# First two projections of v as fp32 products of raw weights, and a new order of all jobs, in a fused attention and MLP block on one core

## The chip, the cores and the metric

The kernel runs on one core of one Trainium2 chip. The metric is the time of one execution on the device, in microseconds (us). TensorE (PE in the profile) multiplies, VectorE (DVE), ScalarE (ACT) and GpSimd (POOL) work element by element, and SyncE (SP) issues nearly all transfers. TensorE writes into PSUM, which the program uses as eight banks of 128x512 fp32, the tiles `dense0` to `dense7`.

## The reference

For x of 2048 rows and 512 columns the output is the sum of three terms; xn is x normalized over each row.

```python
xn = layernorm(x)
return x + A(xn, wq, wk, wv, wo, beta) + B(xn, w1, b1, w2, b2)

# A: 32 heads of 16 columns, 4 segments of 512 rows
q, k, v = xn @ wq, xn @ wk, xn @ wv
for s in range(4):
    p = softmax(q_s @ k_s.T * scale + causal mask)
    o = g * (phi(q_s) @ M) / (phi(q_s) @ z + 1e-6) + (1 - g) * (p @ v_s)
    M += phi(k_s).T @ v_s ; z += sum(phi(k_s))
return concat(o) @ wo

# B: an MLP of width 1792 with a normalization of its own
return gelu(layernorm(xn) @ w1 + b1) @ w2 + b2
```

## The kernel before

**Products in pieces.** A product of fp32 matrices is done in fp16 as three products (`split3`): each operand is scaled by a power of two and split into a high and a low fp16 half, and high times high, high times low and low times high are summed. For K = 512, four blocks of 128, one such product is 12 matmuls. Before a weight can be used it goes through a chain: a load (`w_load`, job `wl`), a measure of its size (`w_square`, job `wm`: for q, k, v and parts of w1 and w2 a product of the weights' upper 16 bits with themselves on TensorE, line L385), a scale worked out of it (`w_scale`, job `wf`, lines L399 and L415), and the split (`w_split`, job `ws`). Of v, pieces 0 and 1 are loaded by one transfer into the room of the later split pieces (the tile `wvs`), and pieces 2 and 3 by two more into a staging tile `pt`.

**The rows.** Blocks of 128 rows are normalized in fp32 (job `X`), transposed on TensorE (`turn`, line L568), and copied out as two fp16 halves, the tile `xnT`. For the first 256 rows there is besides an fp32 copy of the transposed rows, times 1024, in the tile `hzs[1]` (it shares its room with `hT1`): `ln_first`, job `Xf`, copies block 0 by DVE and block 1 by ACT. It serves the first products for k and q (`qk_proj` with `begin`, jobs `Tp 1` and `Tp 0`, line L621), which use raw weights and are scaled afterwards (`qk_first`).

**The products of v.** `v_nat(s, b)`, job `V`, makes v for the 128 rows of block b of segment s: `split3` over the fp16 halves of rows and weights (12 matmuls of 512 columns at line L602), and a copy by ACT into the tile `vt` with a fixed scale (line L723).

**Filler.** 24 jobs `W` (`warm`, line L503) are two matmuls each of an identity matrix with itself, 256 columns wide, whose result nobody reads. They stand at places of the order at the start.

**The order.** All work is cut into 1762 jobs. The string `ORDER` names for each place the stream whose next job comes there, and `BANKS` the PSUM bank of each tile in turn. The jobs are issued in that order, so each engine executes its instructions in the order of the string, and waits only by semaphores for what its instructions need. SP's transfers go through eight semaphores in rotation: a transfer is issued only when the one that used the same semaphore eight transfers ago has landed.

Of the kernel before, what the change touches and what calls it, by code (L numbers as in the profile page):

```python
# [19 lines left out]
P = 128  # L20
D = 512
KT = D // P
# [7 lines left out]
F = 1792  # L30
# [29 lines left out]
def streams():  # L60
# [77 lines left out]


ORDER = (  # L140
    "auhhwhhhlkhhkhhbth7cdaegi7%ghhhbglhf7fh%klhnhs898hkxvhhc%ekhmhd9j&gh9&,&&%gmffn99h9R3gi9R!xrj!((!o!(y()z*CzD+,"
    "))*BCA,)Y)Y+*P-#)-B+-.)*YDo+Y!Y-Y$Y#p-FFF/Z0yz1z$pF-4.-2o0#1F/RBRA2.0:/B1FF2:QF55Y0./FF:5:5Y5513!>F>:254P55>$;"
    ">FFF55;E5GGq>5Y?HGGF3;YHGFHa<5F@II;I?q[IU?GFbGYYF=GG<yHcFGdFYHze;?Hf?Q;IFEUZCzYY=0D14YI3iI<A?2=IJBGGGKYLB0CH1f"
    "GG;MYDHY@PNH2F<F]IOIa=QI]IFFG0?555512FG0G[1YGF5b5FGF@2H]yHZcHYzFBdF0IIze4II55f5F5[BY@[EA1f2J0Y1]5j2KYL55GFG50Y"
    "1GFG2Y50HFFGY1PZ^HMN52FFFHO5y55zz50AQIII^IFFG55a55G_Fb1GC5^iFGEGY5DDHcH55TIiH20I^II1JVGWGYyBP{BY2KG0GzXLMY55NH"
    "1FFG5_Hz5AOCHDUIIDI201IGT2eF55YFGG5YGHFHGHYFF{IIIIFFF55JZ55B0d1fKfB5RFLR5250EMNRFFGOSFGHG1RGG2HFjY0YHIa1bIQIIG"
    "GFSG6F2FPHyG3FcFHSGFzVQIHI4II5zFS6J0W1UB55KYYCLEDXGG3BDYYT55GAMG2VG55HWYN65PH5HIOIIIFeGXF4U55GG5ZH5FFYY3F0GiF5"
    "y1FGdzFzCY20FF1DHIHIBD42IIf01YJ5YYAF2KBY5501555ZT20L15fE2Y055GGF51YFM2GF5555FHN0GHGYFHFI1IQIOIGF63FYY2GFGYHG0V"
    "FGPHy4WaYFII1HIIJ2QZ5055E5zz55XAjK5GGCBGLHMGD1GH5D5Tb55N55BHIOIIIVGG5Yy2GcWFzYGFdYUGXFYPFH0FzH1IHIeIIFF2ABR0RF"
    "1FFfCJ5RD52FfDK5TREjY0155LGGBGY2MHYN5GFGO5SFHFFIZIUHIQIS0G61aFVbi2G50YW15SFG3YP5FFGyFHzG2Uc6F55CSFEXHzDHIQBID0"  # L150
    "eII143d52JTK5YBYGGY5L50GAMGG5HH5N1YH5O624IIIIGF55FGVFY5GHGyWGFF55XPz55BFHFF5Z0H5CD1Y2FFI0IIQB12zIJ0f1U5F6DY5T5"
    "A2KYY3LY0Y12EGFG5M5GFNF55GVFUYZjW5ifY53H5P50YH5OGFF55H1201IIIIXGFFyF2FGC05G12Gz0G5D55F14HY2YHY5HYYZE5D5I4III01"
    "GG250BJKT5LMYYBj55GGGHN1H5H55YFFFIOIIIY2FFGyFzGGYFGFY0HHYGHVFFIQIIZIJC1R5W20FKR515D5XRL5EBUMDT5NGGG205BOSGFFHS"
    "H1FGFHRFF63IIIIGFF2SGVHFGWXyCGH0zUFG1YD65F55555H5SBI2IIED0ITGGHJYK4LYGGM1BGY6YYYNFHFIIHO20IIFVFG555yWFGG1z553H"
    "56GHGFCFZH4FIII20DB1IFX20F355B5JD5YK551525FYYY05YL1YY20MZ15EF2FTG555051GFNG45HOY2FG55GHFFY01HII2IIGFF50515GGF2"
    "H5YG3FG0Y5FHYY12YIZEHII012IG55015J25KG54LGGHM55GNHV5H5OIIIIGWG555GGH0G51H55H5205I12III5JXK5L5555M5N5555OSS6SS6"
    "66"
)


BANKS = (
    "01234567012345670156721657243657435244521654126547302651473026514302561743025613025461372546172354672436517243"
    "06517240362450137524013752031652031467530124763051276340512463052134061352403524075216470521674032164705271064"
    "25710642570165742316574216574031746035720365470347651063547305642713054672130546721304271635046237156024371564"
    "30275162743051260743162074316203120741307413250741653012756301257630125763051724350172501725316754203705432154"
    "70326471503647105437610243716052416035271603457126045712634012563715263471564372156437241560372415602413652413"
    "06524310675243105672431052467045621720415642015620514320561740561743107526104326143726547324657324650246520453"
    "71024573102457312046312573461527340627135436257106257106257301625430162547316254370431625034176240137652407652"
    "04136240173625401732654012736540127365014273654273016427301247013254613720546137205641205637526031753216053216"
    "0532415630415643107546321065341605347165304716054316054732160457162045371625370162534701"  # L170
)


# [13 lines left out]
def infini_mixer_kernel(ctx: ExitStack, tc: tile.TileContext, x, wq, wk, wv, wo, beta, w1, b1, w2, b2, out):  # L187
    nc = tc.nc
    V, A, G, T, Q = nc.vector, nc.scalar, nc.gpsimd, nc.tensor, nc.sync
# [13 lines left out]
    def dense():  # L203
        return dps.tile([P, 512], F32, name="dense" + next(banks), bufs=1)
# [57 lines left out]
    def col(j):  # L262
        return sc[:, j:j + 1]
# [4 lines left out]
    def flat(m):  # L268
        return WT[m].rearrange("p n a c -> p (n a c)").bitcast(F32)

    def piece(m, c):
        n = PIECES[m]
        return flat(m)[:, 512 * c + 1024:512 * c + 1536] if c < n - 2 else stage[m][c - n + 2]
# [115 lines left out]
    def exponents(dst, x):  # L389

        V.tensor_scalar(dst.bitcast(I32), x.bitcast(I32), 1, 0x7F800000, op0=OP.logical_shift_right, op1=OP.bitwise_and)

    def power(dst, h, sign, e):

        V.tensor_scalar(dst.bitcast(I32), h.bitcast(I32), sign, e << 23, op0=OP.mult, op1=OP.add)

    def qk_scale(g0, n):
        p = dense()
        T.matmul(p[:, :2], ones, am[:, :2 * NG].rearrange("p (w g) -> p w g", w=2)[:, :, g0:g0 + 1], start=True, stop=True)  # L399
        h = p[:, 4:6]  # L400
        exponents(h, p[:, :2])
        h = h.unsqueeze(2).to_broadcast([P, 2, n])
        f, s, c = (qksc[:, j, :, g0:g0 + n] for j in range(3))
        power(s, h, -1, 203)
        power(f, h, 1, 64)
        power(c, h, 1, 41)
        V.scalar_tensor_tensor(qkcs[:, g0:g0 + n], f[:, 0], float(2 ** -16), f[:, 1], op0=OP.mult, op1=OP.mult)

    def w_scale(m):
        if m in ("qk", "QK"):  # L410
            return qk_scale(*((0, 1) if m == "qk" else (1, NG - 1)))
        h = m[1:] == "b"
        n = 4 if h else 3 if m == "o" else 1
        p = dense()
        T.matmul(p[:, :n], ones, am[:, AM[m]:AM[m] + n], start=True, stop=True)  # L415
        if m == "1a":
            T.matmul(p[:, 1:2], ones, am[:, 16:17], start=True, stop=True)
        a = p[:, 6:8]
        r = p[:, :1]
        if n > 1:  # L420
            r = a[:, 1:2]
            V.tensor_reduce(r, p[:, :n], axis=AX.X, op=OP.add)
        exponents(a[:, 0:1], r)
        f, s = {"v": (FV, SV), "o": (FO, SO), "1": (F1 + h, S1 + h), "2": (F2 + h, S2 + h)}[m[0]]
        power(col(s), a[:, 0:1], -1, 203)
        power(col(f), a[:, 0:1], 1, 64)
        if m == "o":
            V.scalar_tensor_tensor(col(CO), col(FO), float(2 ** -20), col(FV), op0=OP.mult, op1=OP.mult)
        elif m[0] == "1":
            power(col(CG + h), a[:, 0:1], 1, 41)  # L430
            if not h:
                exponents(a[:, 1:2], p[:, 1:2])
                power(col(FB), a[:, 1:2], 1, 64)
            V.scalar_tensor_tensor(col(B1F + h), col(f), 23.0, col(FB), op0=OP.mult, op1=OP.add)
            b = col(B1F + h).bitcast(I32)
            V.tensor_scalar(b, b, 0x7F800000, None, op0=OP.bitwise_and)
            power(col(SHH + h), col(B1F + h), -1, 267)
        elif m[0] == "2":
            V.scalar_tensor_tensor(col(C2 + h), col(f), float(2 ** -26), col(B1F + h), op0=OP.mult, op1=OP.mult)
# [17 lines left out]
    wqs, wks, wvs, wos, w2s = (WT[m] for m in "qkvo2")  # L457

    FV, SV, FO, SO, CO = range(5)
    F1, S1, F2, S2, CG, SHH, C2, B1F = range(5, 21, 2)  # L460
    FB = 21

    stats = cst.tile([P, 4, 4, 2], F32, name="stats")
    G.memset(stats, 0.0)
# [129 lines left out]
    def x_cols(s, b, k, u):  # L594
        return xnT[:, (2 * s + b // 2) % 3, k, u, P * (b % 2):P * (b % 2) + P]

    def split3(p, ws, xs):

        i = 0
        for k in range(KT):  # L600
            for a, b in ((0, 0), (0, 1), (1, 0)):
                T.matmul(p, ws(k, a), xs(k, b), start=i == 0, stop=i == 3 * KT - 1)  # L602
                i += 1
# [113 lines left out]

    def v_nat(s, b):
        p = dense()
        split3(p, lambda k, a: x_cols(s, b, k, a), lambda k, a: wvs[:, k, a, :])  # L720
        t = vts[b]
        t4 = t.rearrange("p a (b c) -> p a b c", b=3)
        A.activation(t4[:, :, 0:3:2, :], p.rearrange("p (a b c) -> p a b c", b=2, c=DH), AF.Copy,  # L723
                     scale=float(2 ** -16))
        vt[s, b] = t

    def kv(i):
# [161 lines left out]
    hzs = [t.rearrange("p f a c -> p f (a c)").bitcast(F32) for t in hTs]  # L889
# [131 lines left out]
    def e_of(j, a, f):  # L1021
# [12 lines left out]
        "e": e_of,  # L1034
        "A": lambda tok, k: (acc_load, acc_add)[k](tok),
        "wl": w_load, "par": small_loads, "par2": small_use, "zero": zeros, "hold": hold, "const": consts, "wm": w_square, "wf": w_scale, "ws": w_split,
    }
    A.preload_act_table_set("natural_log_exp_and_others")
# [32 lines left out]
```

## Time and profile before

| | |
|---|---|
| time, median of 3 runs (lowest, highest) | 685.41 us (683.58, 686.34) |
| the profiled execution: its own time | 684.2 us |
| its span, first to last instruction | 682.2 us |
| PE busy | 674.6 us, 99% of the span |
| DVE, ACT, POOL busy | 504.9, 492.4, 376.7 us |

The profile is of one execution. Busy of an engine is the time in which it has an instruction under way; matmuls overlap, so that the start of one matmul to the start of the next is a better measure of its cost than its own duration. A line such as L602 is a line of the kernel's file. In the changed file lines from 430 on are 2 higher, and lines after `v_nat` 7 higher.

### The profile page before, as it was taken

Reading aid. Unit: us, or ns where it says so; the run is one execution under the profiler, and the core shown is the slowest. Engines: PE = TensorE matmul, PEld = TensorE weight load, DVE = VectorE, ACT = ScalarE, POOL = GpSimd, SP = SyncE. Lnnn points to the kernel's source line nnn. Section 1 sums busy time; section 2 is a strip of 40 time slices with the busy share of each in tenths; the row PEclk is TensorE's granted clock in tenths of the full one; section 3 lists DMA queues with packets and bytes.
Section 4 is the critical chain, followed back from the end, with each engine's and each line's share of the span. In section 5 each row is a group of like instructions: output and inputs, shape, how many; then the busy total and the mean of one; then the engine's idle time right before and its main releaser. Section 6 shows DMA issues by size and latency. Waiting matters only on the chain.

```text
span 682.2 us, 15538 instructions
## 1 busy us (share of the span) xinstructions
PE 674.6 (99%) x5683; PEld 381.5 (56%) x5683; DVE 504.9 (74%) x1553; ACT 492.4 (72%) x903; POOL 376.7 (55%) x635
## 2 busy tenths in 40 slices
PE   7999999999999999999999999999999999999997
PEld 6765565666555565655455555564655446465543
DVE  5789989987795768887595875997377676878542
ACT  3588999787775659579846848777868565868970
POOL 5386778655645436564743555535553544466662
PEclk8999999999999999999999999999999999999999
DMA  8977342313122141412212224221501323240101
GB/s 280 256 222 170 113 117 66 95 55 73 48 49 71 40 119 36 124 47 50 72 46 56 64 76 97 73 63 32 118 16 35 79 63 80 70 104 17 18 1 61
DMA packets 52887, 55.81 MB, mean 82 GB/s; under 512 B 4990, under 2 KB 41868, under 8 KB 52812
## 3 DMA queue, kind: packets, MB, share of 16 engines
q1 hardware_dynamic: 50508, 50.64, 26.8%
q0 software_dynamic: 2304, 4.20, 3.8%
q8 instruction: 44, 0.72, 0.4%
q14 instruction: 31, 0.25, 0.1%
HBM read 37.77 MB, written 17.05 MB: 80 GB/s over the span
## 4 chain that ended last, share of the span: by engine, by line
PE 97%; DVE 1%; POOL 1%; DMA 0%; issue 0%; ACT 0%; POOLq 0%; DVEq 0%
PE dense L602 40%; PE dense L951 21%; PE dense L832 11%; PE dense L798 6%; PE dense L756 6%; PE dense L971 6%; PE dense L698 2%; PE dense L568 1%; PE dense L385 1%; PE dense L675 1%; PE dense L733 1%; PE dense L503 1%; PE dense L621 1%; DMA xt<-in_A_x_dram 0%; PE dense L769 0%
## 5 line engine op out<-in xcount | busy, mean ns | idle before, releaser
L763 DVE CUSTOM_DVE_ANT_0 dense<-dense,mask 128x384 f32<-128x384 f32 (+3 forms) x512 | 234.3, 522 | 35.2 <-PE dense L756 34.0
L805 ACT ACTIVATE pt<-dense,qkcs 128x512 f32<-128x512 f32 (+1 forms) x384 | 205.4, 624 | 38.1 <-PE dense L798 37.3
L951 PE MATMUL dense<-w2s,hT 128*128 128x512 f16 x672 | 162.9, 380 | 0.0
L602 PE MATMUL dense<-xnT,w1s 128*128 128x256 f16 x1344 | 159.6, 273 | 0.0
L819 POOL TENSOR_SCALAR_AFFINE_SELECT pt<-pt 128x256 f32<-128x256 f32 x256 | 99.0, 419 | 98.8 <-ACT pt L805 98.6
L602 PEld LDWEIGHTS <-w1s 128*128 128x128 f16 x1344 | 128.7, 98 | 29.8 <-issue 8.6
L925 POOL TENSOR_TENSOR hT<-hh,hT 128x512 f16<-128x512 f32 x64 | 67.2, 1050 | 86.9 <-ACT hT L923 85.0
L951 PEld LDWEIGHTS <-hT 128*128 128x128 f16 x672 | 61.3, 98 | 70.6 <-issue 12.9
L832 PE MATMUL dense<-pt,vt 128*32 128x512 f32 (+3 forms) x1024 | 77.6, 436 | 0.0
L763 DVE DVE_READ_ACCUMULATOR2_ANT mc<- 128x1 f32 x512 | 71.1, 139 | 0.1
L904 DVE SCALAR_TENSOR_TENSOR hT<-dense,sc,cb 128x512 f32<-128x512 f32 x64 | 43.4, 679 | 25.4 <-PE dense L602 24.1
L798 PE MATMUL dense<-qst,kst 50*128 50x384 f16 (+3 forms) x512 | 55.0, 298 | 0.0
L832 PEld LDWEIGHTS dense<-pt,vt 128*32 128x32 f32 x1024 | 31.5, 109 | 40.6 <-issue 28.5
L756 PE MATMUL dense<-kst,qst 48*128 48x384 f16 (+3 forms) x512 | 53.1, 298 | 0.0
L921 POOL TENSOR_SCALAR hh<-hT,sc 128x512 f32<-128x512 f32 x64 | 42.5, 663 | 17.4 <-ACT hT L911 10.4
L911 ACT ACTIVATE hT<-hT,b1t 128x256 f32<-128x256 f32 x112 | 46.9, 496 | 1.9 <-DVE hT L904 1.4
L923 ACT ACTIVATE hT<-hh 128x512 f16<-128x512 f32 x64 | 37.0, 578 | 12.1 <-POOL hh L921 12.1
L971 PE MATMUL dense<-wos,oT 128*128 128x512 f16 (+2 forms) x204 | 44.0, 367 | 0.8 <-DVE acc L973 0.7
L602 PE MATMUL dense<-wvs,xnT 128*128 128x512 f16 x192 | 43.7, 379 | 0.0
L602 PE MATMUL dense<-xnT,wks 128*128 128x512 f16 (+1 forms) x240 | 43.0, 331 | 0.0
L602 PE MATMUL dense<-xnT,wqs 128*128 128x512 f16 (+1 forms) x240 | 43.0, 331 | 0.0
L955 DVE SCALAR_TENSOR_TENSOR acc<-dense,sc,acc 128x512 f32<-128x512 f32 x32 | 23.9, 747 | 19.3 <-PE dense L951 19.0
(227 smaller groups left out, 865.4 us busy)
## 6 DMA issues: line engine op xcount, KB each, us to landing
kst<-kd SPq DMA_DIRECT2D x32, 192.0 KB
qst<-qd SPq DMA_DIRECT2D x32, 192.0 KB
qd<-hl SPq DMA_DIRECT2D x36, 128.0 KB
kd<-hl SPq DMA_DIRECT2D x33, 128.0 KB
acc<-in_A_x_dram SPq DMA_DIRECT2D x16, 256.0 KB
acc<-in_B_b_dram POOLq DMA_DIRECT2D x16, 256.0 KB, 4.2
out_dram<-acc SPq DMA_DIRECT2D x15, 256.0 KB
xt<-in_A_x_dram SPq DMA_DIRECT2D x14, 256.0 KB
```

The source lines that it names most:

```text
L602: T.matmul(p, ws(k, a), xs(k, b), start=i == 0, stop=i == 3 * KT - 1)
L756: T.matmul(p[:, o:o + n], stk[i, 0][r, t, P * qb:P * qb + P], stk[i, 1][r, t, :n], start=True, stop=True)
L763: V.tensor_tensor_reduce(p[:, o:o + n], p[:, o:o + n], mask[:, 512 - n:], 1.0, -3e38, OP.add, OP.max, mc[i][:, 4 * b + t, qb:qb + 1])
L798: T.matmul(p[:, o:o + n], stk[i, 1][r, t, P * kb:P * kb + P], stk[i, 0][r, t, P * kb:], start=True, stop=True)
L805: A.activation(pt[i, 4 * b + t][:, OFF[kb]:OFF[kb] + n], p[:, c:c + n], AF.Exp, scale=qkcs[:, i % NG:i % NG + 1])
L819: G.affine_select(v, v, pattern=[[0, 2], [1, P]], compare_op=OP.is_ge, fill=0.0, base=0, channel_multiplier=-1)
L832: T.matmul(p[32 * c:32 * c + 32, P * kb:], vt[s, kb][:, 4 * g + c, 16 * odd:16 * odd + 32], pt[i, 2 * c + odd][:, OFF[kb]:OFF[kb] + LEN[kb ...
L904: V.scalar_tensor_tensor(hz[:, f0:f + 1, :], p[:, :256 * n].rearrange("p (f c) -> p f c", f=n), col(CG + fh), cbt[hf].unsqueeze(1).to_broa ...
L911: A.activation(hz[:, f, :], hz[:, f, :], AF.Gelu_apprx_tanh, bias=b1t[:, fo:fo + 1])
L925: G.tensor_tensor(hT[:, z, 1, :], hht[j, c], hT[:, z, 0, :], op=OP.subtract)
L951: T.matmul(p, t[:, u, P * a:P * a + P], w2s[:, fo, v, :], start=fi == 0 and n == 0, stop=fi == FH - 1 and n == 2)
L971: T.matmul(p[:, c], o[:, u, P * b:P * b + P], wos[:, g, v, c], start=i == 0, stop=i == 3 * NG - 1)
```

## The change

It has two parts. For segment 0 and blocks 0 and 1 `v_nat` no longer uses split weights and split rows: it multiplies the fp32 copy of the rows in `hzs[1]` with the raw fp32 weights of v, four fp32 products of 512 columns for each block, and the copy by ACT scales with a column `SVT`, which `w_scale` works out for v by one more small instruction of DVE. The weights of v are still split, for the other 14 blocks. And `ORDER` and `BANKS` are replaced throughout: the same jobs, as many of each kind, in another order.

```diff
 ORDER = (
-    "auhhwhhhlkhhkhhbth7cdaegi7%ghhhbglhf7fh%klhnhs898hkxvhhc%ekhmhd9j&gh9&,&&%gmffn99h9R3gi9R!xrj!((!o!(y()z*CzD+,"
+    "auhhwhhhlkhhkhhbth7cdhhlhhhhxhih7hehg%kkfhg%f7ja8kg8bcl9%i9smv9R&9d9he9m&nRnh9fh&r!(%jf(g(!(!ggo)yz),)&*C,#)+D"
...
@@ w_scale
-        if m == "o":
+        if m == "v":
+            power(col(SVT), a[:, 0:1], -1, 187)
+        elif m == "o":
...
-    FB = 21
+    FB, SVT = 21, 22
...
     def v_nat(s, b):
         p = dense()
-        split3(p, lambda k, a: x_cols(s, b, k, a), lambda k, a: wvs[:, k, a, :])
+        first = s == 0 and b < 2
+        if first:
+            for k in range(KT):
+                T.matmul(p, hzs[1][:, k, P * b:P * b + P], piece("v", k), start=k == 0, stop=k == KT - 1)
+        else:
+            split3(p, lambda k, a: x_cols(s, b, k, a), lambda k, a: wvs[:, k, a, :])
...
-                     scale=float(2 ** -16))
+                     scale=col(SVT) if first else float(2 ** -16))
```

**TensorE, from the transposition of the first block to the first product for k.** In the rows below the line is followed by what is written and read; `ident` alone is filler (L503 before, L505 after), `xt` the rows, and L385 the measures of weights. Of several equal rows one or two stand. Before:

```order
L503 MATMUL dense1_187<-ident_74 128x256
L568 MATMUL dense2_200<-ident_74,xt_134 128x128 x4
...
L385 MATMUL dense3_211<-wvs_102 128x128
...
L568 MATMUL dense4_220<-ident_74,xt_136 128x128 x4
...
L503 MATMUL dense5_226<-ident_74 128x256
...
L503 MATMUL dense7_232<-ident_74 128x256
L621 MATMUL dense0_242<-hT1_130,wks_101 128x256 x4
```

After:

```order
L505 MATMUL dense3_233<-ident_74 128x256
L570 MATMUL dense4_236<-ident_74,xt_134 128x128 x4
...
L385 MATMUL dense5_242<-wvs_102 128x128
...
L505 MATMUL dense6_259<-ident_74 128x256
...
L570 MATMUL dense7_262<-ident_74,xt_136 128x128 x4
...
L385 MATMUL dense5_242<-pt_201 128x128
...
L399 MATMUL dense0_279<-am_106,ones_79 128x2
L532 MATMUL dense1_287<-ident_74,stats_110 128x128 x2
L623 MATMUL dense2_299<-hT1_130,wks_101 128x256 x4
```

Twenty filler jobs (40 matmuls) stand ahead of the first transposition now, ten before; one stands between the two transpositions, and none behind the second, where there were three. The measure of v's staged pieces (`pt_201`, eight matmuls), the first scale (L399) and two small transpositions (L532) have come ahead of the first product for k.

**TensorE, from there to the second product of v.** After:

```order
L385 MATMUL dense3_320<-wks_101 128x128
...
L415 MATMUL dense6_325<-am_106,ones_79 128x1
...
L385 MATMUL dense4_335<-wqs_100 128x128
...
L385 MATMUL dense3_320<-pt_253 128x128
...
L725 MATMUL dense5_355<-wvs_102,hT1_130 128x512 x2
L725 MATMUL dense5_355<-pt_201,hT1_130 128x512 x2
...
L385 MATMUL dense4_335<-pt_255 128x128
...
L505 MATMUL dense1_373<-ident_74 128x256
...
L725 MATMUL dense7_387<-wvs_102,hT1_130 128x512 x2
```

The two products of v (L725) stand between the measures of k's and q's weights, of which the first two come ahead of v's first product (`wks_101`, `wqs_100`), then one of a staged piece (`pt_253`), and three more between the two. Before, v's products (L602) came after both transpositions of the second pair of row blocks and after all these measures.

**SP, its first transfers.** The names in these rows are the tile written and the input read: `in_A_x` rows, `in_A_wv`, `in_A_wk`, `in_A_wq` weights. Before:

```order
L552 DMA xt<-in_A_x_dram 128x512 x2
L323 DMA wvs<-in_A_wv_dram 128x2x512
L296 DMA wks<-in_A_wk_dram 128x4x128
L296 DMA wqs<-in_A_wq_dram 128x4x128
L552 DMA nN<-in_A_x_dram 128x512
L552 DMA nD<-in_A_x_dram 128x512
L315 DMA pt<-in_A_wv_dram 128x512 x2
L296 DMA wks<-in_A_wk_dram 128x4x128
L296 DMA wqs<-in_A_wq_dram 128x4x128
```

After:

```order
L323 DMA wvs<-in_A_wv_dram 128x2x512
L296 DMA wks<-in_A_wk_dram 128x4x128
L296 DMA wqs<-in_A_wq_dram 128x4x128
L315 DMA pt<-in_A_wv_dram 128x512 x2
L296 DMA wks<-in_A_wk_dram 128x4x128
L296 DMA wqs<-in_A_wq_dram 128x4x128
L296 DMA pt<-in_A_wk_dram 128x4x128
L296 DMA pt<-in_A_wq_dram 128x4x128
L554 DMA nN<-in_A_x_dram 128x512
L554 DMA nD<-in_A_x_dram 128x512
L296 DMA pt<-in_A_wk_dram 128x4x128
L296 DMA pt<-in_A_wq_dram 128x4x128
```

The staged pieces of v have taken the places of the second pair of row blocks (`nN`, `nD`), which now come behind four loads of k's and q's weights, with two more such loads behind them; the 1 MB of `w2s` that was issued between these loads comes after `w1s` now.

## Rows read from the trace of the kernel before

**Rows 1.** The page: busy time of PE; shares of the chain that ended last.

```profile
PE 674.6 (99%) x5683; PEld 381.5 (56%) x5683; DVE 504.9 (74%) x1553; ACT 492.4 (72%) x903; POOL 376.7 (55%) x635
...
PE 97%; DVE 1%; POOL 1%; DMA 0%; issue 0%; ACT 0%; POOLq 0%; DVEq 0%
```

**Rows 2.** Waits of PE: total us, times, longest.

```profile
PE dense L568 <- DVE xt L538: 2.1, 1, 2.1
PE dense L503 <- POOL ident masks.py:199: 1.4, 1, 1.4
PE dense L971 <- DVE acc L973: 0.7, 1, 0.7
```

**Rows 3.** Busy by stretch: PE, PEld, DVE, ACT, POOL; clock, DMA share, GB/s.

```profile
1.40:4.10 2.70, 2.68 (x13) 1.93 (x14) 0.46 (x1) 0.68 (x1) 2.08 (x11) 1.00 0.67 220
4.10:5.10 1.00, 0.97 (x9) 0.60 (x7) 0.97 (x3) 0.00 (x0) 0.00 (x0) 1.00 0.81 237
...
7.50:10.90 3.40, 3.40 (x22) 2.51 (x19) 1.27 (x3) 1.97 (x6) 3.12 (x7) 0.50 1.08 373
...
200.00:300.00 100.00, 100.00 (x855) 58.87 (x853) 73.83 (x220) 67.45 (x123) 48.95 (x84) 1.00 0.29 74
```

**Rows 4.** PE in order of time: start, us, line, tiles, count.

```profile
1.42 3.65 PE L503 MATMUL dense<-ident 128*128 128x256 bf16 x20 [1.42 <-POOL ident masks.py:199]
7.21 0.81 PE L568 MATMUL dense<-ident,xt 128*128 128x128 f32 x4 [2.14 <-DVE xt L538]
...
10.91 1.99 PE L621 MATMUL dense<-hT,wks 128*128 128x256 f32 x8
...
13.32 0.62 PE L385 MATMUL dense<-pt 128*128 128x128 bf16 x8
13.78 0.60 PE L503 MATMUL dense<-ident 128*128 128x256 bf16 x4
...
15.90 0.38 PE L530 MATMUL dense<-ident,stats 128*128 128x128 f32 x2
16.12 1.89 PE L621 MATMUL dense<-hT,wqs 128*128 128x256 f32 x8
17.85 0.38 PE L503 MATMUL dense<-ident 128*128 128x256 bf16 x2
```

**Rows 5.** SP in order of time: issues that had waited for an earlier landing.

```profile
7.90 0.38 SPq L296 DMA_DIRECT2D wqs<-in_A_wq_dram  x1
8.77 0.34 SPq L981 DMA_DIRECT2D zr<-in_A_beta_dram  x1
9.64 0.41 SPq L983 DMA_DIRECT2D mhl<-in_B_b_dram  x1
10.33 0.39 SPq L323 DMA_DIRECT2D w2s<-in_B_w_dram  x1
11.01 0.37 SPq L296 DMA_DIRECT2D pt<-in_A_wk_dram  x1
...
12.47 1.08 SPq L296 DMA_DIRECT2D pt<-in_A_wk_dram  x1
13.59 1.38 SPq L296 DMA_DIRECT2D pt<-in_A_wq_dram  x1
15.02 7.14 SPq L320 DMA_DIRECT2D w1s<-in_B_w_dram  x4
```

**Rows 6.** ACT in order of time: the squares and the second half of the fp32 rows.

```profile
10.19 0.19 ACT L356 ACTIVATION_READ_ACCUMULATOR wqs<-wqs 128x1 f32 x1
10.28 0.58 ACT L575 ACTIVATE hT<-dense 128x512 f32<-128x512 f32 x1
```

**Rows 7.** The chain that ended last, pieces: start, us.

```profile
21.16 2.60 PE dense L602 x12
...
322.93 2.70 PE dense L602 x12
...
355.13 2.59 PE dense L602 x12
```

More of the change, by code (lines that the diff above doesn't have):

```diff
@@ L140 @@
 ORDER = (
-    "auhhwhhhlkhhkhhbth7cdaegi7%ghhhbglhf7fh%klhnhs898hkxvhhc%ekhmhd9j&gh9&,&&%gmffn99h9R3gi9R!xrj!((!o!(y()z*CzD+,"
[L142 to L155, printed above, removed]
@@ L156 @@
-    "H5YG3FG0Y5FHYY12YIZEHII012IG55015J25KG54LGGHM55GNHV5H5OIIIIGWG555GGH0G51H55H5205I12III5JXK5L5555M5N5555OSS6SS6"
-    "66"
+    "auhhwhhhlkhhkhhbth7cdhhlhhhhxhih7hehg%kkfhg%f7ja8kg8bcl9%i9smv9R&9d9he9m&nRnh9fh&r!(%jf(g(!(!ggo)yz),)&*C,#)+D"
+    ")*CB+,*#z-YYBY-+)!)Y-*pAoY+-.DY-Y$Z!F0F/1F2-y.x0FP/12Rz-.#Fz3F$/R0F:.1F5Y3oB5F:B3F:5Y54A20:451/F>2:555!4;>5QFp"
+    "FEP>5;5>5FGqGY$>5GHFGYHGH?F5F?]U?;Ia<IIIG=FGbH3@YY;FG;GcyFdHGF??YQ;<ezHIf=[FfZCaEzY4YYI0@D<AI=BI1G2GHG;JKYBbCG"
+    "[iLGP0<HMNHYDOY5FFI12II?IQFG0@555F1GG=2YG0Fc1?55Hq]FG2FyF[z]FFH@H5IIBZ[IIY5F5ez0J]dYf1KE55Bf5A20YLYY5F1j2MGG01"
@@ new lines @@
+    "5Y20GGFYa5FFGP5i5^H51FFHF5ZNyz2z550IIHQOA^I_I1FGF5{555F2GGHC^0FE^GGYDHDYPT15IIH2_bII0GVGH51J25cyBKWYLGB0GYz5X5"
+    "GF1FUzA5HMH5C5IINODDIIFGT5d{Y2FGG5YHGFGYFFHFIIZjH0IIeFBJF5BK5LR55M55FNRUR5FEFOGS1f26iGGFRfG0FG3YYH1HHIIIIQFG2G"
+    "SHF6FGPyF3GFSHGaFVHQ0zWI1IIB2I0CFzSYJXEY4DKD1YALTYGG5M452bH5GVGWGHH5555Y5IINOIIBFGG55XGFH5YGF5Z5F0FFY6P1c25Uy0"
+    "HzGFFC5HF1FIiIdDII25f0DYB5J1zYU5eFBYKYLEY2T055312Z5f0Y51526GAFGY05F1GaF55M53GFH2G5NHYHF0FI1OIQIIFGFYYGFGYGGVFy"
+    "bFHE5H20154HcWzPYZ2055IQIII1JGKG25j5z5L40C15UA5XeMGBGHGNHD5D5555IHIOTIIV2GGdWYyBFjGY0XHFGY1GHFY2HPFFUIzIIIzBiF"
@@ new lines @@
+    "FfARR5FFFJYCD5Y0K1fFRD2RE5LT5MBGGG5NY5FHGGOS5HFFFIQHIIZISGa0FVW6G55P1S2YH0GFGY13GF2y66bcFzXzHFF55CS30HFIA1IIIB"
+    "UE2D5DJY5YK5GT6G40Y5L5GGHGMY5B3515HNQHIIOIId2GGF55PFV4FUY5GGHWyHFGFZ55zH55FFF50B15CFFDI2I0QIXI1YFJfBi5D25zT0Y1"
+    "52AKEY5LYPYGF0GY5G1FH2GYVFMF5WeZ55555YYNO53HGFF550fHIII1IX20FFGYY1G2F0F12yG0GGCF54HYUE5YzHYIj1DIQHIIJ4BZ2GDGKB"
+    "55T5H555L0555YMGGG5HYN55HFO1FFIIIIYFGFy2G0HGFYY1z2GFFYHYGFV01FWIH2ZIBIIJCDR01UFXKLMRD555N5jT25R5EOG0GHGBS5FGF1"
+    "S2F0FG6HRFF1FIHI20I63IFGSGHFVG4yWzCD6F1GG5H5555FYB5X5DSIIEHITIJGGHYKLYMGGGYYH3BHYNYFOFIII2IFVFGWy501z255GFG55G"
@@ L158 @@
+    "GHF5HCFBFIHZ64II0I1FF235Y505DJ1KXD5Y5YF53250YY1BE5UTYLY55201MFFZG2555FG051H5G2FGY0551FFGHNYIIHOIIF4GF2550152GH"
+    "G0F54YFG1HG25YFYHYYZ0IEIII1G2J01K2G5L5505GG5H55MH5GNHV5IOIIIGG55WXH5GG55G55H51HIIII2550J1K25L55MN5O55555SSS666"
+    "S6"
 )
 BANKS = (
-    "01234567012345670156721657243657435244521654126547302651473026514302561743025613025461372546172354672436517243"
-    "06517240362450137524013752031652031467530124763051276340512463052134061352403524075216470521674032164705271064"
-    "25710642570165742316574216574031746035720365470347651063547305642713054672130546721304271635046237156024371564"
@@ L165 @@
[L165 to L169, printed above, removed]
@@ L170 @@
-    "0532415630415643107546321065341605347165304716054316054732160457162045371625370162534701"
+    "01234567012345670123456701236451706153407651037451637420516374203167420316742167435210743152403714503741520734"
+    "61520374615372406753240673246013524760124375601437560317405361470356174035174035210375162071564203714520672106"
+    "45721064325710643207614307614302671502435072145702146072154201753462015743620157436207543612430756214735061245"
+    "73062174530621307645103764510375641375216307451674351026345102653142563142561307621530215302153027614072614520"
@@ new lines @@
+    "67145206731520637125063412560374123571360517362510462510437610243521407213502714350271437502163750216502731650"
+    "27136052713460523714605234675124765123465723465734165032417632415763264310572640576340514630514630512630521304"
+    "67231476231047623016230475620347516205314762053146205316075163074521074523160745213405721420157632015764320154"
+    "37621534062153406752314067154230671534270165342765013652701632407163507214635072146530146572314675237154637154"
+    "6371057342160731642037156423076047231607423160273426705341267503124750632470635247016352"
```

## The prediction

> **What bounds the kernel.** I read the busy times and the chain that ended last first [rows 1]: TensorE is busy 99% of the span and makes 97% of the chain. Then its waits [rows 2]: three in all. One is the start, 1.4 us; one is the tail, 0.7 us; the only other is 2.1 us before the first transposition, where the normalized rows come late from DVE. By stretch [rows 3] it is busy 100.00 of 100.00 us later on. So the time is TensorE's work plus what it loses at the start, and a change counts only by matmul time added or by time lost at the start.
>
> What is lost at the start is more than the wait. TensorE works from 1.42 on filler; matmuls run at 1.2 GHz at first (13 of 256 columns between 1.40 and 4.10, 0.21 us each), then at 2.4 GHz (9 in 0.97 us, 0.109 each) [rows 3]; the granted clock column shows 1.00 for the first stretch too, so there I go by the durations. Then it stands idle until 7.21 [rows 4], and behind the wait, from 7.5 to 10.9, the granted clock is 0.50 [rows 3]: 3.4 us at half speed, so 1.7 us lost. Wait and clock together cost 2.1 + 1.7 = 3.8 us. That is all the new order can win there, since the first slow stretch from 1.42 stays.
>
> **The products of v.** A split product of v takes 2.60 us (12 matmuls of 512 columns at the full clock [rows 7]). The changed one is four fp32 products of 512 columns, for which before has no row; the nearest is the product of the fp32 rows with raw q weights, four fp32 products of 256 columns, from 16.12 to the next start at 17.85 [rows 4], 1.73 us. With twice the columns that is 3.46 us, so each block costs 0.86 us more, and two cost 1.72. Bounds: below, fp32 columns of the wider form might cost as little as in the split, 0; above, the first product of that kind, from 10.91, whose records span 1.99 [rows 4], would give 3.98 and 2.8 for the two. I take 1.72, since that row was at the full clock from its start.
>
> Perfetto Trace Analysis in the Trainium skill, section Engine Utilization, footnotes the array's output rate with a division by 2 for FP32_LOW_HIGH; if that were the whole price of fp32, one product of v would take half of 3.46. The row of 1.73 us for 1024 columns is four fp16 passes, so this case's trace bears it out only for each of the two records that one fp32 product leaves. What it would give is a rival below.
>
> The extra small DVE instruction and the scale by a column in the ACT copies I cost at nothing: v's copy by ACT has the same size, and neither engine is full in these stretches (from 7.5 to 10.9, DVE 1.27 and ACT 1.97 of 3.40 us [rows 3]).
>
> **The filler moves ahead.** Forty filler matmuls stand before the first transposition instead of twenty. The twenty took until 4.9 (the record of 3.65 us from 1.42 holds the drain of the last [rows 4]); twenty more at 0.109 end at 7.1. The first transposition still waits for the same DVE chain, 7.21 [rows 2, 4]; so the idle 2.1 us are filled and nothing is delayed. Nor is any filler added: the sixteen matmuls fewer that stand between there and the first k product are the gain.
>
> **What is late next.** The measure of v's first pieces needs `wvs`, landed at 7.90 by SP's issues [rows 5]: an issue waits for the transfer eight places earlier, so the issue times 7.90, 8.77, 9.64, 10.33, 11.01 are landings of `wvs`, k, q and the two row blocks; 11.67 is not needed, 12.47 is the second staged piece of v, 13.59 and 15.02 the next k and q loads. In the new order the staged v takes the places of the row blocks, rows of the same size: landed at 10.33 and 11.01. On TensorE: first transposition 7.21 to 7.65, measure 7.90 to 8.36 (8 matmuls of 0.057), filler to 8.58, second transposition to 9.02. Then it is idle until 10.33, and with four matmuls between, again until 11.01; the measure of the staged pieces ends at 11.24, the two small transpositions (15.90 to 16.12 in before, 0.22 [rows 4]) at 11.46; the scale, two products of 2 columns, I leave out on both sides. The k product could not start much sooner without this wait: it needs the fp32 rows' second half from ACT, which now comes behind one of the two fp16 copies; ACT's squares end at 10.38 (0.19 after 10.19), then come two copies of 512 columns, one of which took 0.58 us [rows 6], so 11.5. So it starts at about 11.5, against 10.91 before [rows 4].
>
> By then more is done than before: 16 filler matmuls (1.74 us), the measure of the staged pieces (0.46, from 13.32 to 13.78 [rows 4]), the two transpositions (0.22). That is 2.42 us of work in 0.55 us, a lead of **1.87 us**. It is about the 3.8 us less the new idle 1.75 and the 0.25 before 7.90. The lead rests on the clock staying at full over the two new gaps (1.3 and 0.45 us).
>
> **From there to the split of v's and k's users.** The q and k loads land 0.87 us apart (8.77, 9.64 [rows 5]): from 11.01 on that makes 11.9, 12.8, 13.6, 14.5, then row blocks at 15.2 and 15.9, then the last two at 16.8 and 17.6. TensorE ends the k product at 13.3 and wants them at 13.3, 13.6, 13.9 (fits, closely), then makes v's first product until 17.6 and wants the others at 17.6, 17.8 and 18.3. All fit. I take 0.2 us for the close ones, between nothing and the rival below.
>
> **The order later on.** Matmuls of other array shapes cost at the change of shape: the same 12 matmuls take 2.70 us where the next product has another shape (after 322.93), and 2.59 where not [rows 7]. Counting changes between full, row-halved and column-quartered products in both orders gives 277 before and 278 after: 0.1 us. For new waits behind 50 us I take 0: before has none [rows 2, 3], and the distances in work between makers and readers of scores, softmax and hidden layer are alike in both orders. The upper bound is one wait like the largest seen, 2.1 us [rows 2].
>
> **The sum.** −1.87 + 1.72 + 0.2 + 0.1 = +0.15 us against the profiled execution's own 684.2, so 684.35. That execution lies 1.2 us under the median of the runs shown, 685.41, and within them; so I forecast **685.6 us**. A measurement of this kernel can tell about 0.5% (3.4 us) from no change: this is none.
>
> **Rivals.**
>
> *The clock falls in the new gaps.* Before, it fell after 2.1 us of idle. The gaps are shorter, but between 7.2 and 11.0 TensorE would work only 1.8 of 3.8 us. Then 3.4 us from about 11 on are at half speed, as from 7.5 to 10.9 before [rows 3]: 1.7 us more, 687.3. For it speaks how little work lies there, against it that no single gap reaches the one that did it.
>
> *The loads of k and q come slower, and it ends slower.* Behind the staged v, before's loads of the same kind landed 1.12 and 1.43 us apart (12.47, 13.59, 15.02 [rows 5]), with 1 MB of `w2s` under way beside them, which is moved away. At 1.43 they land at 12.4, 13.9, 15.3, 16.7, and after the row blocks (18.1) at 19.6 and 21.0. Measures in front of v's products wait 1.1, 0.4 and 0.9 us: 2.4 in all, 2.2 over my 0.2, so 687.8; with the clock's 1.7 as well, 689.5, slower by 0.6%. It decides from about 1.0 us apart, where the third load comes after 13.9.
>
> *The fp32 products cost half.* If an fp32 column cost two passes in this form, a product of v would take 1.73, two would save 1.74 instead of costing 1.72: 682.1. This is the case of the footnote of the Trainium skill named above. Against it stands the row of 1.73 us for half the columns [rows 4].
>
> *A wait late in the new order*, at most that of 2.1 us: 687.7, or several of them.
>
> **Chances.** Forecast, with its own range of 684.2 to 686.6, 0.48; clock falls 0.28; slow loads 0.11 (0.07 of it with the clock); half-price products 0.03; a late wait 0.10, half of which is more than one and over 3.4 us. Slower by over 0.5% is 0.07 + 0.05 = 0.12; faster is the half-price case and a chance that the runs stray, 0.04; the rest, 0.84, lies within. For 8 in 10 the range goes from 683.4, under the forecast with the fp32 price at its lower bound (683.9), to 688.4, over the clock falling (687.3), one late wait (687.7) and slow loads alone (687.8).
>
> **What would show it.** Right: no wait of 2.1 us at the first transposition and full clock from about 4 to 11; instead TensorE waits over 1 us for the staged v at about 9 to 11; the k product starts near 11.5; each product of v takes 3.4 to 3.5 us. Wrong: a clock of 0.50 behind the gaps; measures of q's and k's weights waiting for their loads; waits of TensorE behind 50 us.

## The result and the profile after

| | median | lowest, highest | runs |
|---|---|---|---|
| before | 684.26 us | 682.36, 686.34 | 22 |
| changed | 685.81 us | 683.76, 688.07 | 22 |

The ratio is 1.0024, 95% interval 1.0014 to 1.0035: slower by 1.5 us, clear of the noise, but inside the 0.5% that the prediction counts as no change. Here and below, ratios leave out two runs far above all others, one of before (703.35 us) and one of e4 (2422.53 us), which the medians keep. The forecast, 685.6, is 0.2 us off, but by luck: it stood on the median of three runs, 685.41, and added 0.15; the median of 22 runs is 1.15 us lower, and the change costs ten times what was forecast. The profiled execution of the changed kernel took 686.92 us, its span is 685.2.

TensorE is as full as before, 99% [rows 1]; its waits are the view that differs [rows 2]. After, in total us, times, longest:

```profile
PE dense L805 <- DMA qst<-md: 1.5, 1, 1.5
PE dense L505 <- POOL ident masks.py:199: 1.4, 1, 1.4
PE dense L385 <- DMA pt<-in_A_wv_dram: 0.9, 2, 0.6
PE dense L978 <- DVE acc L980: 0.7, 1, 0.7
```

The wait of 2.1 us for `xt` is gone, two short ones for staged pieces of v have come, and one that no sum had: 1.5 us for the maxima that SyncE reads back into `qst`. TensorE in order of time, from the start (which answers to [rows 4]) to the wait:

```profile
1.42 6.59 PE L505 MATMUL dense<-ident 128*128 128x256 bf16 x40 [1.42 <-POOL ident masks.py:199]
7.85 0.60 PE L570 MATMUL dense<-ident,xt 128*128 128x128 f32 x4
...
10.21 0.41 PE L385 MATMUL dense<-pt 128*128 128x128 bf16 x4 [0.59 <-DMA pt<-in_A_wv_dram]
10.94 0.41 PE L385 MATMUL dense<-pt 128*128 128x128 bf16 x4 [0.32 <-DMA pt<-in_A_wv_dram]
...
11.62 1.89 PE L623 MATMUL dense<-hT,wks 128*128 128x256 f32 x8
...
14.24 1.93 PE L725 MATMUL dense<-wvs,hT 128*128 128x512 f32 x4
16.00 1.88 PE L725 MATMUL dense<-pt,hT 128*128 128x512 f32 x4
17.72 0.62 PE L385 MATMUL dense<-pt 128*128 128x128 bf16 x8
...
27.84 1.47 PE L604 MATMUL dense<-xnT,wks 128*128 128x256 f16 x12
29.14 1.08 PE L385 MATMUL dense<-w2s 128*128 128x128 bf16 x16
30.06 1.47 PE L604 MATMUL dense<-xnT,wqs 128*128 128x256 f16 x12
...
67.92 0.39 PE L763 MATMUL dense<-kst,qst 48*128 48x512 f16 x2
69.78 1.02 PE L805 MATMUL dense<-qst,kst 50*128 50x512 f16 x6 [1.47 <-DMA qst<-md]
70.73 2.74 PE L604 MATMUL dense<-xnT,w1s 128*128 128x256 f16 x12
73.26 0.43 PE L415 MATMUL dense<-am,ones 128*128 128x4 f32 x2
```

A product of v goes from 14.24 to 17.72, 3.48 us. The product of normalized rows with `wqs`, at 30.06, is the first place behind the products of v at which TensorE has done the same work in both orders. (At the product with `wks`, at 27.84, it has not: the sixteen matmuls that measure `w2s` are still to come, and in before they are done.) Before:

```profile
18.30 1.08 PE L385 MATMUL dense<-w2s 128*128 128x128 bf16 x16
...
30.16 1.47 PE L602 MATMUL dense<-xnT,wqs 128*128 128x256 f16 x12
```

So the changed kernel is 0.10 us ahead there, with the dearer products of v already paid; the loss comes later. By stretch (columns as in [rows 3]):

```profile
4.10:11.60 7.50, 6.59 (x59) 5.29 (x58) 5.33 (x13) 2.79 (x7) 4.31 (x8) 1.00 1.02 299
54.00:66.00 12.00, 11.99 (x113) 6.66 (x112) 11.03 (x47) 10.22 (x20) 8.92 (x11) 1.00 1.05 258
70.00:72.00 2.00, 2.00 (x13) 1.11 (x13) 1.15 (x4) 1.80 (x4) 0.00 (x0) 0.63 1.04 389
72.00:74.00 2.00, 2.00 (x11) 1.41 (x10) 0.24 (x2) 0.62 (x2) 0.82 (x2) 0.52 0.18 70
```

From 4.1 to 11.6 the clock stays at 1.00; behind the wait it is 0.63 and 0.52 of full over four microseconds, so 0.74 + 0.96 = 1.7 us lost: a loss as large as that of [rows 3] at 7.5, which is gone, now stands at 70. The twelve matmuls at 70.73 show it: 2.53 us to the next start, where as many of the same size at 27.84 take 1.30. Wait and clock less the lead, 1.47 + 1.70 − 0.10 = 3.07 us, are what the two profiled spans differ by, 685.2 − 682.2 = 3.0.

Why the maxima are late stands in SyncE's issues. `md` is written (L781), and read back into `qst` (L786) when the write has landed:

```profile
62.89 0.30 SPq L781 DMA_DIRECT2D md<-mhl  x1
63.24 0.90 SPq L315 DMA_DIRECT2D oT<-in_B_w_dram  x2
66.19 0.59 SPq L786 DMA_DIRECT2D qst<-md  x2
```

The same two in the trace of before:

```profile
63.60 0.30 SPq L774 DMA_DIRECT2D md<-mhl  x1
64.99 0.55 SPq L779 DMA_DIRECT2D qst<-md  x2
```

The changed kernel issues the write 0.7 us earlier and the read-back 1.2 us later: 3.3 us from one to the other instead of 1.39. Two things differ. The new order has put a load of w2 (`oT`, 512 KB) between the two. And it has moved two loads of `acc` and their additions of b2 (accumulating transfers of GpSimd's queue) ahead of them, so that the DMA engines' share is still 1.05 from 54 to 66; in the trace of before it falls to 0.06 from 64 to 66:

```profile
64.00:66.00 2.00, 2.00 (x15) 0.71 (x13) 1.63 (x8) 1.97 (x6) 1.29 (x2) 1.00 0.06 14
```

### The profile page after: what moved, and what is told of

It reads as the page before. It is cut to its first block, busy times and chain, and to the rows that moved or that the text cites. A ratio compares the mean times of both kernels' runs of the same rounds, so it can differ in the third digit from the quotient of the medians.

```text
span 685.2 us, 15499 instructions
## 1 busy us (share of the span) xinstructions
PE 677.1 (99%) x5675; PEld 382.6 (56%) x5675; DVE 506.6 (74%) x1554; ACT 491.6 (72%) x903; POOL 377.6 (55%) x635
## 4 chain that ended last, share of the span: by engine, by line
PE 91%; DVE 4%; DMA 2%; ACT 1%; issue 1%; SPq 0%; POOL 0%; POOLq 0%; DVEq 0%
PE dense L604 37%; PE dense L958 20%; PE dense L839 11%; PE dense L805 6%; PE dense L978 6%; PE dense L763 6%; DVE dense L770 2%; PE dense L700 2%; PE dense L725 1%; DMA pt<-in_A_wv_dram 1%; PE dense L570 1%; PE dense L385 1%; PE dense L677 1%; DMA qst<-md 1%; PE dense L623 1%
## 5 line engine op out<-in xcount | busy, mean ns | idle before, releaser
L839 PE MATMUL dense<-pt,vt 128*32 128x256 f32 (+3 forms) x1024 | 77.6, 436 | 0.1
L874 POOL TENSOR_TENSOR nN<-nN,oT 128x512 f32<-128x512 f32 x16 | 20.3, 1268 | 33.2 <-DVE oT L872 33.2
L604 PE MATMUL dense<-wvs,xnT 128*128 128x512 f16 x168 | 38.0, 379 | 0.0
```

Source lines behind the costliest of these rows:

```text
L839: T.matmul(p[32 * c:32 * c + 32, P * kb:], vt[s, kb][:, 4 * g + c, 16 * odd:16 * odd + 32], pt[i, 2 * c + odd][:, OFF[kb]:OFF[kb] + LEN[kb ...
```

## The experiments

In the diffs `ORDER.insert(j, ORDER.pop(i))` moves the job at place i to place j. The first four ran on one chip with 36 runs of before (684.23), e5 to e7 with 17 (684.32), e8 and e9 with 23 (684.38).

**e1: the changed kernel, with the load of w2 earlier, so that it no longer stands between write and read-back.**

```diff
+ORDER = list("".join(ORDER))
+for i, j in ((219, 164),):
+    ORDER.insert(j, ORDER.pop(i))
```

> The changed kernel with one job moved: the load of the last two pieces of w2 stands ahead of the second unit's k, so SP issues it some 15 us earlier and not between the write and the reading back of the row maxima. Theory A (the late wait and the half clock behind it make the changed kernel slower): no wait of TensorE on the reading back, scores start near 68.3 us instead of 69.8, clock 1.00 throughout behind the start, profile span near 682.0 and time within 0.1% of before (about 684.3). Theory B (the start and the price of the fp32 products make it slower, the wait is made up later): time as the changed kernel, 1.0024 of before, 685.8.

Measured: 687.26 us, ratio 1.0038 (1.0024 to 1.0052). SyncE's issues:

```profile
62.15 0.30 SPq L785 DMA_DIRECT2D md<-mhl  x1
66.08 0.55 SPq L790 DMA_DIRECT2D qst<-md  x2
```

With nothing between them the read-back is 3.9 us behind the write, so it is not the load of w2 that holds up the write. The time fits neither theory, A's 684.3 or B's 685.8. The wait for `qst` itself is nearly gone (0.2 us); TensorE waits for VectorE instead, 0.7 us for `mst` and 1.5 us for `mc`. VectorE in order of time shows why:

```profile
65.43 2.68 DVE L455 SCALAR_TENSOR_TENSOR wqs<-pt,qksc,wqs 128x512 f16<-128x512 f32 x1
68.03 0.18 DVE L747 COPY mst<-dense 128x32 f32<-128x32 f32 x1
```

and GpSimd at the same time:

```profile
64.82 0.87 POOL L944 DMA_DIRECT2D acc<-in_B_b_dram  x1 [3.03 <-DMA acc<-in_A_x_dram]
65.44 0.98 POOL L457 TENSOR_SCALAR w1s<-w1s,sc 128x512 f32<-128x512 f32 x1
66.11 1.45 POOL L461 TENSOR_TENSOR wks<-pt,wks 128x512 f16<-128x512 f32 x1
```

A product that takes 0.74 us elsewhere took 2.68 beside two of GpSimd's, and the copy of `mst` and the maxima stand behind it. It hangs on hundredths of a microsecond: in the changed kernel's trace the product with `wqs` starts at 65.47 and GpSimd's scaling of `w1s` at 65.53, and the product takes 0.81. The clock is 1.00 in this execution; eight of e1's twelve runs have a mean clock of 0.998 or less.

**e2: the changed kernel, with the loads of `acc` and the additions of b2 behind the read-back; the load of w2 stays between.**

```diff
+ORDER = list("".join(ORDER))
+for i, j in ((183, 221), (200, 221), (189, 221), (210, 221),):
+    ORDER.insert(j, ORDER.pop(i))
```

> The changed kernel with the loads of the second and third block of x into acc, and the two adds of b2 by POOL's queue, moved behind the reading back of the row maxima; the load of w2 stays between write and reading. Theory A1 (what counts is the w2 load between the two on SP's queue): the wait stays over 1.0 us, time as the changed kernel. Theory A2 (what counts is all the traffic still under way when the maxima are written): the write lands in under 2 us instead of 3.3, the wait falls under 0.5 us, and time to about 684.5.

Measured: 683.69 us, ratio 0.9992 (0.9980 to 1.0005). SyncE's issues:

```profile
62.63 0.30 SPq L785 DMA_DIRECT2D md<-mhl  x1
62.98 0.90 SPq L319 DMA_DIRECT2D oT<-in_B_w_dram  x2
64.06 0.58 SPq L790 DMA_DIRECT2D qst<-md  x2
```

1.43 us, as before. The scores start at 67.89 without a wait, and the clock does not fall behind them. By the medians this takes back 2.1 us of the changed kernel's time, and the rest of the change is level with before.

**e3: the kernel before, with only that load of w2 moved between write and read-back.**

```diff
+ORDER = list("".join(ORDER))
+for i, j in ((159, 208),):
+    ORDER.insert(j, ORDER.pop(i))
```

> The kernel before with one job moved the other way: the load of the last two pieces of w2 from some 12 us ahead to right behind the write of the row maxima. Theory A: the wait appears, 1 to 1.5 us on the reading back, in some executions with 3.4 us of half clock behind it: 1.0015 to 1.0045 of before. Theory B: no difference, within 0.05%.

Measured: 685.13 us, ratio 1.0012 (0.9999 to 1.0025). The write takes 1.60 us to the read-back (62.88, 64.48), but TensorE waits for what is read:

```profile
PE dense L802 <- DMA qst<-md: 1.1, 1, 1.1
```

So in this execution the load of w2 seems to cost something, on the read-back that is queued behind it and not on the write. By the times it cannot be told from nothing. In e2 the same order of transfers shows no wait; its read-back was issued 0.4 us sooner and its scores stand 0.7 us later on TensorE than here.

**e4: the kernel before, with only the fp32 products of v, in v's old places** (two splits of v moved behind them, since they write over the raw weights).

```diff
+ORDER = list("".join(ORDER))
+for i, j in ((71, 99), (71, 99),):
+    ORDER.insert(j, ORDER.pop(i))
...
+        first = s == 0 and b < 2
+        if first:
+            for k in range(KT):
+                T.matmul(p, hzs[1][:, k, P * b:P * b + P], piece("v", k), start=k == 0, stop=k == KT - 1)
```

> The kernel before with the two fp32 products of v, scaled when copied, in their old places of the order; only the splits of v's third and fourth piece come later, since they overwrite the raw weights. Price by the row of four fp32 products of 256 columns: 0.86 us for each, 1.72 for both, so 1.0025 of before (686.0). Theory B needs more than the lead of the new start, over 3 us (1.0045). If fp32 columns cost half: 1.7 us faster.

Measured: 685.83 us, ratio 1.0026 (1.0011 to 1.0042): the products cost 1.8 us by the ratio, with an interval of 0.8 to 2.9. The half-price rival, which would have made this faster by 1.7, falls. The size is better read from the trace, since eight of the eleven runs in the ratio have a mean clock of 0.998 or less, and six of the 35 of before: from start to next start the two products take 3.53 and 3.61 us here, and 2.59 and 2.68 in the trace of before, so 1.87 more.

**e5: the changed kernel, with only the additions late, the loads of `acc` early.**

```diff
+ORDER = list("".join(ORDER))
+for i, j in ((201, 221), (212, 221),):
+    ORDER.insert(j, ORDER.pop(i))
```

> After the change, with the two additions of b2 to acc (A 1 1 and A 2 1, accumulating transfers of GpSimd's queue, 6 to 9 us each from issue to landing in the changed kernel's trace) moved behind the read-back of the maxima; the two loads of acc on SyncE's queue (issued at 52.8 and 57.4) stay early. Theory C (the additions alone hold up the write of md): the read-back is issued within 2 us of the write, the wait L805 <- qst is gone, 683.4 to 684.2 us, as with loads and additions both late. Theory D (any transfers under way do it, the loads as well): the read-back is still 2.5 us or more behind the write, a wait of 0.8 us or more is left, 685.0 to 686 us.

Measured: 686.67 us, ratio 1.0039 (1.0024 to 1.0053). The read-back is back to 1.76 us behind the write (62.33, 64.09), as theory C has it; the time is above even D's. TensorE waits 0.8 us for `mc` and 0.4 for `qst`. VectorE and GpSimd in order of time:

```profile
64.64 2.39 DVE L455 SCALAR_TENSOR_TENSOR wqs<-pt,qksc,wqs 128x512 f16<-128x512 f32 x1
66.96 0.18 DVE L747 COPY mst<-dense 128x32 f32<-128x32 f32 x1
```

```profile
63.51 1.78 POOL L944 DMA_DIRECT2D acc<-in_B_b_dram  x2
64.69 1.79 POOL L461 TENSOR_TENSOR wks<-pt,wks 128x512 f16<-128x512 f32 x1
```

It is the collision of e1 again, at another time: the two issues, from 63.51 on, now stand ahead of GpSimd's product, which starts at 64.69, beside VectorE's. That explains the waits, not the whole of 686.67: its profile's span, 683.6, is 1.6 us below that of the changed kernel, whose runs are faster. Five of its seven runs had a mean clock of 0.996 to 0.998, and the profiled one, at 0.999, shows 1.00 in every stretch from 4 to 78 us, so part of it may be clock lost in executions that no trace shows.

**e8: as e5, with the additions issued behind GpSimd's product.**

```diff
+ORDER = list("".join(ORDER))
+for i, j in ((201, 234), (212, 234),):
+    ORDER.insert(j, ORDER.pop(i))
```

> As e5, with the two additions of b2 issued still later: behind GpSimd's product for wks (the group ahead of the scale of 2b) instead of right behind the read-back. In e5 GpSimd's two issues (63.51 to 65.29) pushed its wks product to 64.69, beside VectorE's product for wqs (64.64), which took 2.39 us instead of 0.70; the maxima mc of the second unit came 1.6 us late by it and TensorE waited 0.8 us for them. Theory I (what e5 gained on the read-back it lost to that collision of VectorE and GpSimd): the wqs product takes 0.7 to 0.8 us, no wait for mc of 0.5 us or more is left, and the time falls from 686.7 to 683.4 to 684.4 us. Theory J (the early loads of acc still cost something by themselves): 685 us or more, with a wait of TensorE for the read-back or for acc.

Measured: 684.41 us, ratio 0.9995 (0.9979 to 1.0010). On GpSimd the product now comes first, and on VectorE its neighbour has its old length:

```profile
64.20 1.17 POOL L461 TENSOR_TENSOR wks<-pt,wks 128x512 f16<-128x512 f32 x1
65.31 1.77 POOL L944 DMA_DIRECT2D acc<-in_B_b_dram  x2
```

```profile
65.38 0.74 DVE L455 SCALAR_TENSOR_TENSOR wqs<-pt,qksc,wqs 128x512 f16<-128x512 f32 x1
```

No wait for `mc` is left, 0.2 us for `qst`. Two jobs moved on by thirteen places are worth 2.3 us against e5 by the medians: theory I, at the upper end of its range (684.4). The early loads of `acc` cost nothing that can be measured; the additions were the cost, once by the write that waits behind them, and once by GpSimd's issues.

**e6: e2, with the memset of `kst` on GpSimd moved away from the first normalization** (one run; the diff is against e2).

```diff
 ORDER = list("".join(ORDER))
-for i, j in ((183, 221), (200, 221), (189, 221), (210, 221),):
+for i, j in ((183, 221), (200, 221), (189, 221), (210, 221), (28, 46),):
```

> The version with late acc loads (e2), and the memset of kst on GpSimd (zero 0) moved behind the row broadcast Cb 0, so that no memset runs beside the first normalization on VectorE. Theory E (VectorE's tensor_scalar is slowed by GpSimd's memset beside it): the two tensor_scalar of xt at 6.4 us take 1.0 us together instead of 2.4. Theory F (they are slow for where they stand, waiting for their rows of x): still above 2 us. The time stays within 0.3% of e2's 683.7 us either way, since TensorE has warm-up products until 7.9 us and then waits for pieces of v.

Measured: 684.31 us in one run, span 682.6 against e2's 682.7. VectorE's two normalizations in e2, and here:

```profile
6.51 2.42 DVE L544 TENSOR_SCALAR xt<-xt,ag,stats 128x512 f32<-128x512 f32 x2 [0.74 <-POOL stats L495]
```

```profile
6.67 1.00 DVE L544 TENSOR_SCALAR xt<-xt,ag,stats 128x512 f32<-128x512 f32 x2 [0.74 <-POOL stats L495]
```

Theory E: the memset beside them cost VectorE 1.4 us, in one execution each. **e9**, the same kernel timed, shows what that is worth.

> The version with late acc loads and additions (e2) and the memset of kst moved behind Cb 0 (e6's order), now timed: 683.4 to 684.0 us, ratio to before 0.998 to 1.0002, within 0.1% of e2's 0.9992, since TensorE waits at neither of the places where VectorE was slowed by the memset. If VectorE's 1.4 us were worth something on the path, it would come out at 682.5 us or below.

Measured: 684.08 us, ratio 0.9997 (0.9988 to 1.0006): nothing. In its trace TensorE waits 1.4 us for staged pieces of v, against 0.6 in e2; in e6, the same kernel, it waited 0.2, so this wait differs from execution to execution.

**e7: e2, with three filler products moved from 18 to 23 us into the idle time before the staged pieces of v.**

```diff
+ORDER = list("".join(ORDER))
+for i, j in (..., (68, 43), (76, 44), (79, 45),):
+    ORDER.insert(j, ORDER.pop(i))
...
+    letters = "".join(BANKS)
+    banks = iter(letters[:24] + "103" + letters[24:31] + letters[32] + letters[34:36] + letters[37:])
```

> The version with late acc loads (e2), and three warm-up products (W 21, 22, 23, 0.23 us each) that stand at 17.9, 21.9 and 22.7 us moved ahead of the squares of v's second piece, where TensorE waits 0.22 and 0.35 us for the pieces. Theory G (the start's time on TensorE goes straight through to the end, as the forecast of the change assumed): 0.69 us less work behind 13 us, 0.0 to 0.15 us lost ahead of it, so 0.5 to 0.7 us below e2: 683.1 us, ratio to before 0.9984. Theory H (the gain is taken by the next wait, for a scaled weight or for DMA): as e2, ratio 0.9992, with a new wait in the pages of waits between 20 and 70 us.

Measured: 683.87 us, ratio 0.9995 (0.9986 to 1.0004): theory H, with the new wait at 18 us, a little ahead of the stretch that it named. TensorE in order of time:

```profile
18.54 0.41 PE L390 MATMUL dense<-pt 128*128 128x128 bf16 x4 [0.56 <-DMA pt<-in_A_wq_dram]
```

In this execution the 0.69 us taken out came back as 0.56 us of waiting for q's weights, so at 18.5 us the start is bound by its loads here. No version here beats before by more than the measurement can tell; e2 has the lowest time, 683.69.

## Why the prediction was right, and where it was not

**The start: right, to 0.15 us.** As the text had it, no wait is left at the first transposition, the staged v is waited for at 9.6 to 10.9 us, the k product starts at 11.62 (forecast: about 11.5), and the clock stays at 1.00 over the gaps. The fillers took longer (6.59 us from 1.42, so the first transposition came at 7.85, not 7.21): the slow stretch at the start lasted longer in this execution, with 6 matmuls between 4.4 and 5.4 us and 11 between 6.4 and 7.4. TensorE waited for the staged pieces behind it anyway. The loads of q and k had no wait. All this with the products of v paid leaves a lead of 0.10 us at 30.06, where the sum has −1.87 + 1.72 + 0.2 = +0.05, a loss. The clock's fall in the new gaps and the slow loads, two rivals of 0.28 and 0.11, didn't come in the profiled execution.

**What the start's sum took from one execution.** The clock's fall at 7.5, 1.7 of the 3.8 us that the prediction counts as lost, need not come. e3 and e4 keep the start of before; their waits for `xt`, first e3 and then e4:

```profile
PE dense L572 <- DVE xt L542: 1.5, 1, 1.5
```

```profile
PE dense L574 <- DVE xt L544: 1.8, 1, 1.8
```

and the stretch from 7.5 to 10.9 of each:

```profile
7.50:10.90 3.40, 2.74 (x25) 2.34 (x25) 2.11 (x5) 2.67 (x7) 3.13 (x7) 1.00 1.07 376
```

```profile
7.50:10.90 3.40, 2.54 (x25) 2.14 (x23) 1.91 (x5) 2.64 (x7) 3.11 (x7) 1.00 1.08 371
```

The clock stays at 1.00, and TensorE waits 0.7 and 0.9 us more for the fp32 rows. The product with `wqs` starts at 29.47 and 31.32, which is 29.45 without e4's 1.87: 0.7 us sooner than in the trace of before, and 0.6 sooner than the changed kernel's 30.06 (e1 and e2, with that kernel's start, reach it at 29.31 and 29.80). Of 75 runs of before in the ratios of the experiments, 59 have a mean clock of 0.999 or 1.000, where 1.7 us lost of 682 would leave 0.998 or less. So the start came out as summed against an execution that is not the usual one.

**The price of fp32: right.** 3.48 and 3.49 us a product where 3.46 was forecast; against 2.59 and 2.68 in before that is 1.70 us for the two, where 1.72 was. e4 shows 1.87 in its trace and 1.8 in its times, with a wide interval.

**The order later on: the step that failed** is "For new waits behind 50 us I take 0". Its argument was the distance in work between makers and readers. That is not shorter: from the transposition of the maxima on TensorE to the first scores it is 5.5 us before (62.31 to 67.84) and 6.8 after (61.52 to 68.31, without the wait). The argument looked at the engines and not at the transfers that the order puts ahead of a small one. A wait of TensorE behind 50 us was one of the signs of being wrong that the prediction named. The price of the rival "a wait late in the new order", 687.7 for the largest wait seen, covers the 686.92 of the profiled execution; it had a chance of 0.10, and the clock's fall that can follow such a wait was priced only at the start: 1.5 us of wait and 1.7 of clock stand in this trace. Over the runs it is less. Nine of the 22 runs have a mean clock of 1.000, and their median is 685.29; of before's 36, sixteen have, with 683.80: 1.5 us, about the wait alone. The runs with a lower clock come on top of it: seven of the 22 have 0.998 or less, with a median of 687.19. e2, which removes wait and fall together, is 2.1 us under the changed kernel by the medians.

**What causes it.** e1 excludes the load of w2 as what holds up the write; e2, e5 and e8 show that it is the additions of b2 under way. The landings go with it: the second addition, issued at 59.84, landed at 65.9 (6.1 us later), and the read-back was issued at 66.19; in e1 they stand at 65.8 and 66.08. Why the write lands late behind them, in the queues or in the memory, no run here tells apart. Nor does a run tell how e2's 0.5 us under before (within its interval) divides between lead and price: e4 and e2 together would put the lead at 2.3 us, with an uncertainty of more than 1 us, and the two profiled executions put it at 1.8 (1.70 + 0.10).

## What to carry to other kernels

When all jobs get a new order, look at each small transfer on which a product waits, a write and read-back above all, and list what the new order puts under way ahead of it on every queue; the distance in work between maker and reader doesn't show it. Before taking a wait away by moving a job, look at what the moved job's engine does at the new place: e1 and e5 traded the wait for a collision of two other engines. A short wait on TensorE can cost as much again by the clock behind it, but not in every execution: before a loss in one profile is counted as won, look whether the mean clocks of the other runs show it too.

## What the runs showed of the hardware

- A small write (16 KB) was read back 3.3 and 3.9 us after its issue, when it had landed, with two accumulating transfers of GpSimd's queue issued ahead of it (256 KB each, 6.1 to 8.5 us from issue to landing), and 1.4 to 2.1 us after with all but the first of them moved behind it.
- The clock fell to half at about 70.5 us behind a wait of 1.47 us, and at 7.5 in before behind one of 2.1. It did not behind waits of 1.8 us (e4) and 1.5 us (e3) at the same place of the start, nor over gaps of 0.59 and 0.32 us, nor in the profiled execution of e1, where TensorE waited four times between 67.5 and 70.9, 0.91 us at most. The length of the wait alone doesn't decide it.
- VectorE's 128x512 normalization takes 0.50 us alone and 1.2 beside GpSimd's memset; its product of two SBUF tiles 0.74 us alone, and 2.39 and 2.68 beside GpSimd's products. The Trainium skill, SBUF — State Buffer, section SBUF: two separate sides, says that the two engines share a pair of ports as an exclusive lock, held for a whole instruction, among other cases when VectorE's instruction has two SBUF inputs and GpSimd's reads SBUF; whichever starts first gets it. The lengths of the product agree with the lock; the order of the starts does not in e5, where VectorE's is shown to start 0.05 us sooner and still takes 2.39.
